# Pooled attention into a gated MLP: PSUM banks by turns in blocks 5 to 8, operands on one address remainder, and a new order of the steps

## The chip, the cores and the metric

The kernel runs on one core of one Trainium2 chip. Its time is the device time of one execution in microseconds (us), and a kernel's time is the median of several executions. Profiles, waits and clocks come from one further execution under the hardware profiler.

## The reference

```python
k_p = k.reshape(B, H, Sp, 8, D).mean(axis=3)          # B, H, S, D = 8, 8, 576, 64; Sp = 72
v_p = v.reshape(B, H, Sp, 8, D).mean(axis=3)
scores = q @ k_p.T / sqrt(D)
attn = exp(scores - max) / (sum + 1e-9)
x = (attn @ v_p) as 4608 tokens x 512
xn = x / sqrt(mean(x*x) + 1e-6) * rms_g
g, val = xn @ w_gate, xn @ w_val                      # 512 -> 1536 each
out = (g * sigmoid(g) * val) @ w_out                  # 1536 -> 512
```

All in float32.

## The kernel before, in words

The 4608 tokens are handled in nine blocks of 512 tokens (block 0 to block 8). The attention of a batch (576 tokens) is worked out in four pairs of heads and gives the tokens of about one block; it runs ahead of the MLP blocks that use it. The hidden width of 1536 is cut into twelve tiles f of 128 (written 0 to 9, a, b).

Accuracy comes from splitting: every float32 operand y of the MLP is stored as y_hi (rounded to float32r) and y_lo = y - y_hi, and a product is made of three float32r matmuls: hi x hi, lo x hi, hi x lo. All big matmuls have a 128x128 stationary operand and 512 moving columns.

**Blocks 0 to 4.** For each tile f: `mm1` twice (steps mg and me, 12 matmuls each, line 812; stationary the weights W1, moving the tokens xh, xl), which fill PSUM banks 2 and 3; `gate` (gt, ScalarE Silu out of bank 2), `val` (vl, VectorE product with bank 3), `act_hi` (hi, ScalarE, line 834), `act_lo` (lo, VectorE, line 839), then `mm2` (mo, 12 matmuls, line 853; stationary the activation hh or hl, moving the weights W2), which accumulates four output tiles in banks 4 to 7 over all twelve f. After the last tile `o_copy` (ev, line 867) takes the banks out and `o_store` (st) sends them to memory.

**Blocks 5 to 8.** They are worked in two pairs, (5, 6) and (7, 8), and the first projection of a pair is done for both blocks at once by seven half-size products a tile in place of eight (steps pr`<i><f><k>`, k = 0 to 6, six matmuls each, function `product`, line 764). X collects products 0, 2 and 4 in one PSUM bank (px), Y the products 1, 3, 5 and 6 in another (py). VectorE and ScalarE combine them (cp, u2, sa, u3, c2, sw, v2, v1, va, vb, lines 908 to 917): `v1` and `va` make the odd block's activation from product 6, the last one; `vb` leaves the even block's activation in an SBUF tile `hb` that holds all twelve tiles. The odd block's `mm2` of tile f is done in two halves (mp) among the products of tile f+1; that of the last tile (mo5b, mo7b) follows the last product. Then the even block has only its twelve `mm2` (mo60 to mo6b, mo80 to mo8b) from the stored `hb`.

**PSUM.** The eight banks are given by number: attention in banks 0 and 1, X in 2, Y in 3, output tiles of every block in 4 to 7 (lines 756, 758, 844). A step such as `av730:1` overrides the bank.

**SBUF.** Tiles are laid out pool after pool, each rounded up to 32 bytes a partition. `const.tile([P, 104])` on line 208, named "rest", is read by nobody and takes 416 bytes a partition. In this layout the start addresses, taken by 256, leave these remainders: the weights W1, W2 and the split tokens xp of blocks 5 to 8 (which lie in freed W1 slots) 0; xh, xl, the ring of eight buffers for the products' weights, act, hl and the pool tile "st" 128; hh and the transposed probabilities 192.

**hh and hl.** hh has two buffers; hl has one, and for odd f of an even block (6, 8) `act_lo` uses the one act buffer in place of it (line 837).

**The order of the work** is written out by hand in two strings, `ORDER` (block 0 and the attention it needs) and `LATER` (all else, 2072 steps). The function `run` issues the steps one after the other; each engine executes its own in that order, and SyncE issues all DMAs in that order too. The attention's steps are sc (scores, PE), mx, sb, sm (VectorE), ex (ScalarE Exp), nm (GpSimd), tr (VectorE transpose), dm (12 DMAs that place the transposed probabilities), av (PE), xc, xd (copies), sq, jn (squares and their sum); the token norm's are sh, sl, rm (PE), rt (ScalarE Sqrt), rc (VectorE reciprocal, line 540), rs (VectorE scaling, line 547); the pair's operands are made by ys, yh, yl; rl loads a product's weights.

Of the kernel before, what the change touches and what calls it, by code (L numbers as in the profile page):

```python
# [92 lines left out]
sm221 wf03 ex220 wd0 wh03 sm220 wl01 lv23 nm221 ws01 av210:0 gt14 nm220 pk23 av211:1 wl03 me14 lq23 xd21 xc210 ws03
xc211 mo13 vl14 hi14 pv23 wh04 wl04 mg15 lo14 ws04 wh02 wl02 sc23:01 ws02 sq21 tr22 gt15 jn21 me15 dm22 mx230 sb230
mx231 ex230 sb231 mo14 vl15 ex231 sm230 hi15 lo15 nm230 sm231 mg16 nm231 lk30 tr23 me16 gt16 dm23 av220:0 vl16
av221:1 pk30 xc220 hi16 mo15 xd22 xc221 sq22 lo16 jn22 mg17 lq30 lv30 wt1 me17 gt17 wf10 sc30:01 vl17 wd1 wf11 wh11
hi17 pv30 wl11 mo16 lk31 wh13 wf12 ws11 mx301 lv31 wl13 lo17 wf13 ws13 mx300 mg18 sb300 sb301 ex300 av230:0 ex301
# [15 lines left out]
sb421 sb420 ex421 pv42 me28 gt28 sm421 nm421 mo27 ex420 vl28 lk43 hi28 sm420 lv43 wt5 mg29 lo28 pk43 nm420 av410:0
lq43 gt29 wf50 av411:1 wf51 me29 wd5 xd41 xc410 wf52 pv43 xc411 wh53 wf53 wh51 wl53 sq41 sc43:01 vl29 wl51 ws53 hi29
jn41 ws51 mo28 mx431 lk50 mx430 lo29 mg2a wh52 wl52 wh54 wl54 ws52 ws54 tr42 me2a gt2a sb431 dm42 pk50 ex431 sb430
mo29 vl2a ex430 sm431 hi2a sm430 nm431 lo2a mg2b nm430 tr43 me2b dm43 gt2b mo2a xh33 vl2b xh31 xl33 xh32 xl31 xh30
av420:0 xl32 hi2b av421:1 xl30 xc420 xc421 lo2b mg30 lv51 kt3 lq50 xd42 lv50 me30 gt30 sc50:01 vl30 pv50 hi30 mo2b
lk51 mx501 lo30 wd6 mx500 sb500 mg31 ev21 ev22 ex500 sb501 st21 st22 pk51 lq51 ex501 av430:0 sm500 gt31 av431:1
sm501 nm500 me31 xd43 nm501 xc430 pv51 xc431 ev23 sq42 tr50 st23 jn42 ev20 dm50 vl31 mo30 sq43 hi31 jn43 lo31 mg32
sh4 sl4 rm40:0 gt32 rm41:1 me32 rt40 st20 rt41 rc40 lv52 wt6 sc51:01 vl32 mo31 lk52 rs40 hi32 wf60 wf61 wh61 wl61  # L120
wh63 lo32 mg33 wl63 ws61 rc41 wf62 ws63 wf63 me33 rs41 gt33 mx511 wh62 wh64 sb511 wl62 mo32 vl33 ex511 wl64 ws62
mx510 sb510 ws64 pk52 hi33 av500:0 sm511 ex510 lq52 av501:1 xc500 lo33 nm511 mg34 xc501 xd50 sm510 sq50 wd7 pv52
# [835 lines left out]
```

## Time and profile before

| | |
|---|---|
| median of 3 runs | 1043.09 us (1041.45 to 1043.99) |
| the profiled execution: its time, its span | 1040.0 us, 1037.9 us |
| mean granted TensorE clock | 0.976 |
| busy: PE, DVE (VectorE), ACT (ScalarE), POOL (GpSimd) | 1007.0, 632.0, 449.3, 227.4 us |

PE's rows are TensorE's matmuls, PEld its weight loads. In a row of the timeline the columns are: start, duration in us, engine, line, operation, tile written <- tiles read, shape, count, and in brackets the idle time of the engine just before with what ended it. The duration of one matmul in the profile (about 0.4 us) covers its way through the array; matmuls follow one another much closer than that, so their pace is read from start to start.

### The profile page before, as it was taken

The page shows a single profiled execution, that of the slowest core. Times are in us where ns is not written, and L with a number is a line of the kernel's source. Part 1 is how long each engine was busy: PE and PEld are TensorE (multiplying, and loading weights), DVE is VectorE, ACT ScalarE, POOL GpSimd, SP SyncE. Part 2 cuts the span into 40 slices and gives each one's busy share as a digit, 9 for nine tenths or more (in the row PEclk, how much of TensorE's full clock was granted, in tenths as well). Part 3 has the DMA queues.
Part 4 walks back from the last instruction along what each step waited for, and adds up shares of the span by engine and source line. Part 5 has one row for each costly group of instructions (what it writes and reads, how often), then busy time and mean ns, then how long its engine had stood idle before and what let it go on. Part 6 is the DMA issues. An engine that isn't in the chain of part 4 may idle for free.

```text
span 1037.9 us, 13861 instructions
## 1 busy us (share of the span) xinstructions
PE 1007.0 (97%) x4850; PEld 790.9 (76%) x4850; DVE 632.0 (61%) x1024; ACT 449.3 (43%) x845; POOL 227.4 (22%) x216
## 2 busy tenths in 40 slices
PE   7999999999999999999999999999999999999987
PEld 6777777777777777777777787878786778888866
DVE  6699996554772964775485385644655764444432
ACT  5767665543473454554364362322333432111121
POOL 2314440144333541355324140000000000000000
PEclk7599999999999999999999999999999999999999
DMA  9345422245345353444244323564544134544311
GB/s 303 126 158 187 171 73 77 71 139 143 102 134 156 100 159 91 140 145 150 83 146 147 97 89 115 162 206 143 167 143 134 41 122 146 151 149 144 102 40 41
DMA packets 97077, 134.71 MB, mean 130 GB/s; under 512 B 10225, under 2 KB 60145, under 8 KB 95729
## 3 DMA queue, kind: packets, MB, share of 16 engines
q1 hardware_dynamic: 97008, 133.83, 41.3%
q8 instruction: 39, 0.64, 0.2%
q14 instruction: 30, 0.24, 0.1%
HBM read 91.23 MB, written 34.60 MB: 121 GB/s over the span
## 4 chain that ended last, share of the span: by engine, by line
PE 86%; DVE 7%; ACT 2%; issue 2%; DMA 1%; SPq 0%; ACTq 0%; DVEq 0%
PE psg L812 28%; PE po L853 26%; PE py L764 13%; PE px L764 10%; PE pss L390 4%; PE psx L471 3%; DVE wt L258 1%; PE pst L447 1%; DVE wt L262 1%; DMA main<-kT 1%; PE psr L555 1%; DVE wt L254 1%; DVE w L280 0%; ACT prob L368 0%; PE psb L579 0%
## 5 line engine op out<-in xcount | busy, mean ns | idle before, releaser
L812 PE MATMUL psg<-xh,w 128*128 128x512 f32 x960 | 304.4, 399 | 1.8 <-ACT act L819 1.8
L853 PE MATMUL po<-w,hh 128*128 128x512 f32 x864 | 227.4, 395 | 0.0
L812 PEld LDWEIGHTS psg<-xh,w 128*128 128x128 f32 x960 | 177.4, 188 | 50.7 <-issue 5.3
L853 PEld LDWEIGHTS po<-w,hh 128*128 128x128 f32 x864 | 163.9, 190 | 36.8
L812 PE MATMUL psg<-xl,w 128*128 128x512 f32 x480 | 189.3, 395 | 0.2 <-DVE xl L642 0.2
L764 PE MATMUL py<-xp,wp 128*128 128x512 f32 x576 | 149.7, 395 | 0.8 <-DVE u L914 0.8
L853 PE MATMUL po<-w,hl 128*128 128x512 f32 x432 | 126.9, 403 | 9.8 <-DVE hl L839 5.1
L764 PEld LDWEIGHTS py<-xp,wp 128*128 128x128 f32 x576 | 108.3, 188 | 27.2 <-DVE u L914 1.2
L764 PE MATMUL px<-xp,wp 128*128 128x512 f32 x432 | 112.7, 396 | 0.0
L812 PEld LDWEIGHTS psg<-xl,w 128*128 128x128 f32 x480 | 90.2, 188 | 21.9 <-DVE xl L642 0.6
L853 PEld LDWEIGHTS po<-w,hl 128*128 128x128 f32 x432 | 79.8, 189 | 34.0 <-DVE hl L839 6.5
L421 POOL TENSOR_TENSOR prob<-prob,sm 128x360 f32<-128x360 f32 x48 | 43.7, 911 | 282.4 <-DVE sm L417 279.9
L764 PEld LDWEIGHTS px<-xp,wp 128*128 128x128 f32 x432 | 81.0, 188 | 20.0 <-ACT xraw L479 0.5
L824 DVE TENSOR_TENSOR act<-act,psg 128x512 f32<-128x512 f32 x60 | 40.8, 681 | 81.7 <-PE psg L812 70.1
L834 ACT CAST hh<-act 128x512 fp32r<-128x512 f32 x84 | 52.1, 621 | 66.0 <-DVE act L824 57.2
L839 DVE TENSOR_TENSOR hl<-act,hh 128x512 fp32r<-128x512 f32 x78 | 58.3, 748 | 34.3 <-ACT hh L834 26.7
L819 ACT ACTIVATE act<-psg 128x512 f32<-128x512 f32 x60 | 35.8, 597 | 67.7 <-PE psg L812 64.1
L819 ACT ACT_TABLE_LOAD x34 | 43.6, 1283 | 38.0 <-DVE hl L839 19.9
L911 DVE TENSOR_TENSOR u<-u,py 128x512 f32<-128x512 f32 x24 | 16.5, 688 | 67.4 <-PE py L764 67.4
L516 POOL TENSOR_TENSOR acc<-acc,sq 128x576 f32<-128x576 f32 x21 | 31.5, 1499 | 102.4 <-ACT sq L510 102.4
L913 ACT ACTIVATE hb<-hb 128x512 f32<-128x512 f32 x24 | 15.2, 632 | 87.8 <-DVE hb L912 87.8
L686 POOL TENSOR_TENSOR wt<-wsum,wt 128x256 fp32r<-128x256 f32 x48 | 38.3, 814 | 53.1 <-ACT wt L682 53.0
(132 smaller groups left out, 1225.0 us busy)
## 6 DMA issues: line engine op xcount, KB each, us to landing
wp<-sum SPq DMA_DIRECT2D x96, 256.0 KB
wp<-blocks SPq DMA_DIRECT2D x72, 256.0 KB
blocks<-w SPq DMA_DIRECT2D x24, 512.0 KB
sum<-wt SPq DMA_DIRECT2D x48, 256.0 KB
wx<-w SPq DMA_DIRECT2D x10, 1024.0 KB
v<-vN SPq DMA_DIRECT2D x32, 288.0 KB
out<-o SPq DMA_DIRECT2D x36, 256.0 KB
wx<-w SPq DMA_DIRECT2D x16, 512.0 KB
```

Of the source, the lines that this page charges most:

```text
L390: nc.tensor.matmul(s["ps", h][:, t * SP:(t + 1) * SP], s["q"][r, o:o + P], s["pk"][r, :], start=True, stop=True)
L421: nc.gpsimd.tensor_tensor(l_pr(h), l_pr(h), sm[:, :, None].broadcast_to([P, len(OFFS2), SP]), ALU.mult)
L471: nc.tensor.matmul(ps[r, :n], s["pv"][:, r], x, start=True, stop=True)
L516: nc.gpsimd.tensor_add(acc[b], acc[b], st[b, p]["sq"])
L686: nc.gpsimd.tensor_sub(y[:, 1], place(f, f"T{k}"), y[:, 0].bitcast(F32))
L764: nc.tensor.matmul(ps[:, :NB], w[:, a, c, :], x[:, b, c, :], start=j == 0 and not more, stop=j == len(todo) - 1, skip_group_check=more)
L812: nc.tensor.matmul(ps[:, :NB], w[:, c, cols], x[c], start=(j == 0), stop=(j == len(todo) - 1))
L819: nc.scalar.activation(t, ps[:, :NB], AF.Silu)
L824: nc.vector.tensor_mul(t, t, ps[:, :NB])
L834: nc.scalar.copy(a, act_in(i, f))
L839: eng.tensor_sub(l, act_in(i, f), hh[i, f].bitcast(F32))
L853: nc.tensor.matmul(po[i][t], x[i, f][:, t * P:(t + 1) * P], w, start=(f == 0 and k == 0), stop=(f == NF - 1 and k == 2))
```

## The change

Three things are changed. No step is added or taken out: `LATER` holds the same 2072 steps.

1. **Banks by turns.** X and Y of pair (7, 8) go to banks 4 and 5; the output tiles of block 6 go to banks 0 to 3, those of block 7 to 6, 7, 0, 1 and those of block 8 to 2 to 5. The even block's first step, mo60 or mo80, now stands ahead of the odd block's last step mo5b or mo7b, with its hi60/lo60 (hi80/lo80) among the products of the last tile. `act_lo` of an even block's tile 0 goes to a buffer of the pool tile "st".
2. **Addresses.** The unused "rest" tile is gone (416 bytes less ahead of everything), `pk` is padded from 72 to 96 elements (2 buffers, 96 bytes more each) and the four tiles "mxe" from 80 to 128 bytes (32 bytes more each after rounding). The start addresses by 256 become: W1, W2 and xp 0 - 416, xh, xl, ring, act, hl and "st" 128 - 416 + 128, hh 192 - 416 + 128 + 192. All of these leave the remainder 96.
3. **A new order.** The first 29 steps of `LATER` are the same; from there on it differs. In blocks 1 to 4 the attention's steps stand at other places among the tiles. The attention of batch 7 is done by tile 4 of block 5 (before: by the end of block 5), its token norm (rm7 to rs7) in tile 5 of block 5 (before: during mo60 to mo64), and half of the operands yh7, yl7 are made in the last tile of block 5.

```diff
+BANK1 = {5: (2, 3), 7: (4, 5)}
+BANK2 = {6: (0, 1, 2, 3), 7: (6, 7, 0, 1), 8: (2, 3, 4, 5)}
...
-    const.tile([P, 104], F32, name="rest")
...
-            pk = sb2.tile([P, SP], F32, tag="pk", name=f"pk{b}_{p}")
+            pk = sb2.tile([P, 96], F32, tag="pk", name=f"pk{b}_{p}")[:, :SP]
...
-            x = sb1.tile([P, 2, 2, n], F32, tag=f"mxe{p}", name=f"mx{b}_{p}")
-            s["mx"], s["sm"] = x[:, 0], x[:, 1]
+            x = sb1.tile([P, 2, 2, 8], F32, tag=f"mxe{p}", name=f"mx{b}_{p}")
+            s["mx"], s["sm"] = x[:, 0, :, :n], x[:, 1, :, :n]
...
-            st["X"] = bank(2, f"px{i}_{f}_{k}")
+            st["X"] = bank(BANK1[i][0], f"px{i}_{f}_{k}")
         elif k in (1, 3, 5):
-            st["Y"] = bank(3, f"py{i}_{f}_{k}")
+            st["Y"] = bank(BANK1[i][1], f"py{i}_{f}_{k}")
...
     def act_lo(i, f, eng):
-        tag = "act" if second(i) and f % 2 else "hl"
-        l = hl[i, f] = sb1.tile([P, NB], F32R, tag=tag, name=f"hl{i}_{f}")
+        if second(i) and f == 0:
+            l = sb2.tile([P, NB], F32R, tag="st", name=f"hl{i}_{f}")
+        else:
+            l = sb1.tile([P, NB], F32R, tag="act" if second(i) and f % 2 else "hl", name=f"hl{i}_{f}")
+        hl[i, f] = l
...
-            po[i] = [bank(4 + t, f"po{i}_{t}") for t in range(NB // P)]
+            po[i] = [bank(k, f"po{i}_{t}") for t, k in enumerate(BANK2.get(i, (4, 5, 6, 7)))]
```

The order at the end of block 5, before and after:

```
... pr5b5 c25b rl705 sw5b mp5a1 rl706 v25b vb5b pr5b6 av730:0 rl710 v15b av731:1 va5b xc730 xc731 xd73 hi5b sq73 lo5b
jn73 mo5b hi60 lo60 sh7 sl7 mo60 hi61 ev52 ev51 ev50 st52 ev53 st51 lo61 st50 st53 rm71:0 hi62 rm70:1 mo61 ...

... u25b hi60 mp5a0 ... pr5b3 lo60 ... c25b pr5b5 sw5b yl72 mp5a1 rl706 v25b vb5b pr5b6 mo60 rl710 v15b va5b
hi5b lo5b mo5b hi61 lo61 mo61 hi62 ev52 ev53 ev50 st52 ev51 st53 lo62 st50 st51 mo62 ...
```

and in tile 5 of block 5, after:

```
pr550 rl560 v154 va54 rm70:1 rl561 cp55 rm71:0 pr551 hi54 rt71 lo54 pr552 rl562 u255 rt70 rc71 mp540 rl563 sa55 pr553 rc70
pr554 rl564 u355 rl565 c255 pr555 rs70 sw55 mp541 rl566 v255 vb55 pr556 rs71 pr560 ...
```

More of the change, by code (lines that the diff above doesn't have):

```diff
@@ L93 @@
[L93 to L97, printed above, removed]
@@ L113 @@
[L113 to L117, printed above, removed]
@@ L118 @@
[L118 to L122, printed above, removed]
@@ L163 @@
-nm731 mp591 rl5b6 v25a sw5a tr73 pr5a6 dm73 vb5a pr5b0 v15a va5a pr5b1 cp5b hi5a pr5b2 lo5a u25b mp5a0 sa5b pr5b3
-rl700 pr5b4 rl701 u35b rl702 rl703 rl704 pr5b5 c25b rl705 sw5b mp5a1 rl706 v25b vb5b pr5b6 av730:0 rl710 v15b
-av731:1 va5b xc730 xc731 xd73 hi5b sq73 lo5b jn73 mo5b hi60 lo60 sh7 sl7 mo60 hi61 ev52 ev51 ev50 st52 ev53 st51
-lo61 st50 st53 rm71:0 hi62 rm70:1 mo61 rt71 lo62 rt70 rc71 mo62 hi63 lo63 rc70 mo63 hi64 lo64 rs70 mo64 hi65 lo65
-rs71 mo65 hi66 ys73 yh72 yh71 lo66 yl72 mo66 hi67 yh73 lo67 yl71 yh70 mo67 hi68 yl70 lo68 ys74 mo68 hi69 lo69 yh74
@@ L183 @@
-pr7a3 pr7a4 rl7b4 u37a pr7a5 rl7b5 c27a sw7a mp791 rl7b6 v27a vb7a pr7a6 pr7b0 v17a va7a pr7b1 cp7b hi7a pr7b2 lo7a
-u27b mp7a0 sa7b pr7b3 pr7b4 u37b pr7b5 c27b sw7b mp7a1 v27b vb7b pr7b6 v17b va7b hi7b lo7b mo7b hi80 lo80 mo80 hi81
-ev72 ev71 ev70 st72 ev73 st71 lo81 st70 st73 mo81 hi82 lo82 mo82 hi83 lo83 mo83 hi84 lo84 mo84 hi85 lo85 mo85 hi86
-lo86 mo86 hi87 lo87 mo87 hi88 lo88 mo88 hi89 lo89 mo89 hi8a lo8a mo8a hi8b lo8b mo8b ev83 ev82 ev81 ev80 st83 st82
-st81 st80
+pv22 dm21 me13 gt13 wt0 sc22:01 wf00 vl13 wf01 wh01 hi13 mo12 mx220 wf02 wh03 sb220 wf03 lo13 ex220 wl01 wd0 mx221
@@ new lines @@
+mx320 sb320 mx321 ex320 sb321 me20 lk33 lv33 gt20 sm320 ws24 nm320 mo1b ex321 vl20 pk33 hi20 sm321 lq33 mg21 ev13
+ev12 nm321 st13 lo20 st12 tr32 me21 gt21 dm32 ev10 ev11 av310:0 vl21 av311:1 xc310 hi21 mo20 xd31 xc311 pv33 lo21
+sq31 sc33:01 jn31 st11 mg22 st10 mx330 lk40 mx331 sb331 lv40 wt3 sb330 ex331 me22 gt22 sm331 wd3 wf30 nm331 av320:0
+pk40 ex330 wf31 av321:1 vl22 lq40 wf32 mo21 xd32 hi22 wf33 sm330 xc321 wh34 lo22 nm330 xc320 pv40 wh32 wl34 mg23
+wl32 ws34 sq32 ws32 jn32 me23 gt23 wh31 wh33 wl31 mo22 vl23 wl33 ws31 hi23 ws33 tr33 mg24 lo23 lv41 dm33 sc40:01
@@ new lines @@
+gt24 me24 mx401 mx400 sb400 sb401 ex400 mo23 vl24 ex401 lk41 sm400 hi24 sm401 nm400 mg25 lo24 nm401 tr40 pk41 dm40
+av330:0 gt25 av331:1 me25 xd33 xc330 pv41 xc331 sq33 mo24 vl25 jn33 hi25 lo25 sh3 mg26 lq41 sl3 wd4 wt4 rm30:0 gt26
+lv42 rm31:1 me26 rt30 wf40 rt31 rc30 wf41 wh41 av400:0 wf42 wh43 av401:1 xc400 wf43 vl26 mo25 xc401 wl43 rs30 hi26
+wl41 ws43 ws41 lo26 mg27 xd40 rc31 pv42 wh44 sc41:01 gt27 wl44 rs31 me27 ws44 lk42 wh42 wl42 mx410 sq40 sb410 ws42
+mo26 mx411 ex410 vl27 sb411 hi27 sm410 ex411 mg28 lo27 nm410 sm411 pk42 nm411 me28 lq42 gt28 tr41 dm41 mo27 vl28
@@ new lines @@
+hi28 lo28 sc42:01 mg29 mx421 sb421 mx420 ex421 sb420 lk43 lv43 me29 gt29 sm421 wt5 ex420 av410:0 vl29 av411:1 pk43
+nm421 mo28 hi29 sm420 lq43 wf50 xc410 wd5 xc411 xd41 wf51 lo29 wh51 nm420 wh53 pv43 mg2a wl53 wf52 ws53 sq41 wl51
+jn41 ws51 sc43:01 gt2a wf53 me2a lk50 mx430 mx431 wh52 mo29 wh54 wl52 vl2a wl54 hi2a ws52 pk50 ws54 lo2a lq50 mg2b
+tr42 sb430 dm42 sb431 ex430 me2b gt2b sm430 nm430 mo2a xh33 vl2b xh32 xl33 xh30 xl32 xh31 xl30 lv50 hi2b xl31 ex431
+lo2b mg30 kt3 sm431 nm431 av420:0 gt30 tr43 av421:1 me30 xd42 dm43 xc420 pv50 xc421 sq42 sc50:01 vl30 jn42 hi30 mo2b
@@ new lines @@
+mx500 mx501 lo30 sb500 sb501 ex500 mg31 ev20 lk51 ev22 st20 ex501 st22 sm500 wd6 me31 sm501 wt6 gt31 lv51 pk51 ev23
+nm500 av430:0 lq51 vl31 ev21 st23 av431:1 wf60 hi31 st21 mo30 nm501 xd43 xc430 xc431 wf61 lo31 wf62 wf63 mg32 pv51
+me32 wh63 gt32 wl63 wh61 ws63 wl61 ws61 mo31 vl32 hi32 lo32 wh62 mg33 wl62 wh64 ws62 wl64 ws64 sq43 tr50 me33 jn43
+gt33 dm50 sh4 sl4 mo32 vl33 hi33 lo33 rm40:0 rm41:1 rt40 mg34 lv52 rt41 rc40 me34 gt34 rs40 av500:0 wt7 vl34 av501:1
+xc500 rc41 hi34 mo33 xc501 wf70 lo34 wf71 wh71 xd50 rs41 wl71 mg35 wh73 wl73 ws71 wd7 wf72 pv52 sq50 ws73 wf73
@@ new lines @@
+mo38 xc520 hi39 lo39 wh82 av521:1 wh83 wl82 mg3a xc521 xd52 wl83 ws82 pv60 ws83 sq52 jn52 tr53 me3a gt3a dm53
+sc60:01 vl3a hi3a mo39 mx600 mx601 lo3a sb601 sb600 ex601 mg3b lk61 ex600 lv61 sm601 me3b sm600 nm601 gt3b nm600
+tr60 av530:0 xh43 vl3b dm60 av531:1 xh41 xl43 mo3a xh42 xl41 xh40 xl42 hi3b xl40 xc530 xc531 lo3b mg40 xd53 pv61
+pk61 sq53 me40 gt40 jn53 lq61 wd9 sh5 lv62 wt9 mo3b sl5 kt4 vl40 wf90 hi40 rm50:0 ev30 rm51:1 ev31 wf91 mg41 lo40
+rt50 st30 wf92 st31 wf93 rt51 rc50 me41 gt41 ev32 rc51 ev33 st32 sc61:01 st33 vl41 mo40 lk62 mx611 hi41 sb611 wh94
@@ new lines @@
+lo41 ex611 wl94 rs51 av600:1 ws94 mg42 wh93 xc600 wl93 mx610 sm611 ws93 sb610 nm611 av601:1 wh92 pk62 gt42 wl92 me42
+rs50 lq62 ws92 xc601 wh91 pv62 ex610 wl91 mo41 vl42 ws91 xd60 hi42 sm610 sq60 lo42 nm610 mg43 tr61 dm61 sc62:01 gt43
+me43 mx620 mx621 wta sb621 sb620 ex621 mo42 vl43 wfa0 ex620 sm621 hi43 wfa1 sm620 wha1 nm621 lk63 wha3 mg44 lo43
+nm620 wda wla3 lv63 wfa2 wsa3 me44 wfa3 gt44 wla1 pk63 wsa1 lq63 av610:0 vl44 av611:1 xc610 hi44 mo43 xd61 xc611
+lo44 pv63 mg45 wha2 wha4 wla2 wla4 wsa2 wsa4 sq61 tr62 sc63:01 gt45 jn61 dm62 me45 mx630 sb630 mx631 ex630 sb631
@@ new lines @@
+mo44 vl45 ex631 sm630 hi45 lo45 nm630 sm631 mg46 nm631 lk70 lv70 me46 gt46 tr63 dm63 mo45 vl46 hi46 pk70 lo46
+av620:0 av621:1 xc620 mg47 xc621 xd62 pv70 lq70 me47 gt47 lv71 sq62 jn62 av630:0 vl47 av631:1 xc630 wdb hi47 mo46
+xd63 xc631 lo47 pv71 mg48 sq63 wtb sc70:01 gt48 jn63 me48 lk71 mx700 wfb0 sb700 sh6 mx701 wfb1 ex700 sl6 wfb2 mo47
+sb701 wfb3 whb3 vl48 ex701 wlb3 sm700 hi48 wsb3 whb2 sm701 nm700 rm60:0 mg49 lo48 wlb2 rt60 pk71 nm701 wsb2 lq71
+tr70 whb1 rm61:1 wlb1 gt49 rc60 me49 dm70 rt61 rs60 mo48 whb4 vl49 wlb4 rc61 hi49 sc71:01 lo49 mg4a mx710 wsb4 wsb1
@@ new lines @@
+rs61 lk72 lv72 me4a ys53 gt4a ys54 yh52 mo49 vl4a yh51 yl52 hi4a yh50 mg4b lo4a yl51 yh53 yh54 yl50 me4b gt4b yl53
+yl54 mo4a rl500 rl501 ys56 rl502 rl503 rl504 rl505 vl4b yh56 rl506 ys55 rl510 pr500 hi4b pr501 lo4b rl511 cp50 yh55
+yl56 pr502 rl512 u250 mp4b0 yl55 rl513 sa50 mx711 pr503 sb711 pk72 ex711 pr504 rl514 u350 lq72 sb710 av700:1 rl515
+c250 ex710 av701:0 sm711 xc700 sw50 pr505 sm710 nm711 xd70 mp4b1 nm710 rl516 v250 xc701 sq70 vb50 pr506 ev41 ev40
+pv72 st41 pr510 st40 rl520 v150 sc72:01 va50 rl521 cp51 tr71 hi50 pr511 lk73 lo50 ev43 lv73 dm71 mx720 pr512 ev42
@@ new lines @@
+pr533 sq72 dm73 pr534 u353 jn72 pr535 c253 sw53 mp521 v253 vb53 pr536 pr540 v153 va53 rl544 pr541 cp54 rl545 hi53
+rl546 rl550 pr542 lo53 rl551 rl552 u254 mp530 rl553 sa54 pr543 av730:1 rl554 u354 av731:0 xc730 pr544 xc731 xd73
+sq73 pr545 jn73 rl555 c254 sw54 mp531 rl556 v254 sh7 vb54 pr546 sl7 pr550 rl560 v154 va54 rm70:1 rl561 cp55 rm71:0
+pr551 hi54 rt71 lo54 pr552 rl562 u255 rt70 rc71 mp540 rl563 sa55 pr553 rc70 pr554 rl564 u355 rl565 c255 pr555 rs70
+sw55 mp541 rl566 v255 vb55 pr556 rs71 pr560 rl570 v155 rl571 cp56 va55 pr561 hi55 pr562 lo55 rl572 u256 mp550 rl573
@@ new lines @@
+sa56 pr563 pr564 rl574 u356 pr565 rl575 c256 sw56 mp551 rl576 v256 vb56 pr566 pr570 rl580 v156 va56 pr571 rl581 cp57
+hi56 pr572 lo56 rl582 u257 mp560 rl583 sa57 pr573 pr574 rl584 u357 pr575 rl585 c257 sw57 mp561 rl586 v257 vb57 pr576
+pr580 rl590 v157 va57 pr581 rl591 cp58 hi57 pr582 lo57 rl592 u258 mp570 rl593 sa58 pr583 pr584 rl594 u358 pr585
+rl595 c258 sw58 mp571 rl596 v258 vb58 pr586 pr590 rl5a0 v158 va58 pr591 rl5a1 cp59 hi58 pr592 lo58 rl5a2 u259 mp580
+rl5a3 sa59 pr593 pr594 rl5a4 u359 pr595 rl5a5 c259 sw59 mp581 rl5a6 v259 vb59 pr596 pr5a0 rl5b0 v159 va59 pr5a1
@@ new lines @@
+rl5b1 cp5a hi59 pr5a2 lo59 rl5b2 u25a mp590 rl5b3 sa5a pr5a3 pr5a4 rl5b4 u35a pr5a5 rl5b5 c25a sw5a mp591 rl5b6 v25a
+vb5a pr5a6 pr5b0 rl700 v15a va5a pr5b1 rl701 cp5b hi5a pr5b2 yh70 lo5a rl702 u25b hi60 mp5a0 yl70 rl703 sa5b yh71
+pr5b3 lo60 yl71 pr5b4 rl704 u35b rl705 yh72 c25b pr5b5 sw5b yl72 mp5a1 rl706 v25b vb5b pr5b6 mo60 rl710 v15b va5b
+hi5b lo5b mo5b hi61 lo61 mo61 hi62 ev52 ev53 ev50 st52 ev51 st53 lo62 st50 st51 mo62 hi63 lo63 mo63 hi64 lo64 ys73
+mo64 hi65 lo65 yh73 ys74 mo65 hi66 yl73 yh74 lo66 yl74 mo66 hi67 lo67 ys76 mo67 hi68 ys75 yh76 lo68 yh75 yl76 mo68
@@ new lines @@
+rl780 v176 va76 pr771 rl781 cp77 hi76 pr772 lo76 rl782 u277 mp760 rl783 sa77 pr773 pr774 rl784 u377 pr775 rl785 c277
+sw77 mp761 rl786 v277 vb77 pr776 pr780 rl790 v177 va77 pr781 rl791 cp78 hi77 pr782 lo77 rl792 u278 mp770 rl793 sa78
+pr783 pr784 rl794 u378 pr785 rl795 c278 sw78 mp771 rl796 v278 vb78 pr786 pr790 rl7a0 v178 va78 pr791 rl7a1 cp79 hi78
+pr792 lo78 rl7a2 u279 mp780 rl7a3 sa79 pr793 pr794 rl7a4 u379 pr795 rl7a5 c279 sw79 mp781 rl7a6 v279 vb79 pr796
+pr7a0 rl7b0 v179 va79 pr7a1 rl7b1 cp7a hi79 pr7a2 lo79 rl7b2 u27a mp790 rl7b3 sa7a pr7a3 pr7a4 rl7b4 u37a pr7a5
@@ L188 @@
+rl7b5 c27a sw7a mp791 rl7b6 v27a vb7a pr7a6 pr7b0 v17a va7a pr7b1 cp7b hi7a pr7b2 lo7a u27b hi80 mp7a0 sa7b lo80
+pr7b3 pr7b4 u37b pr7b5 c27b sw7b mp7a1 v27b vb7b pr7b6 mo80 v17b va7b hi7b lo7b mo7b hi81 lo81 mo81 hi82 ev70 ev71
+ev72 st70 ev73 st71 lo82 st72 st73 mo82 hi83 lo83 mo83 hi84 lo84 mo84 hi85 lo85 mo85 hi86 lo86 mo86 hi87 lo87 mo87
+hi88 lo88 mo88 hi89 lo89 mo89 hi8a lo8a mo8a hi8b lo8b mo8b ev83 ev82 ev81 ev80 st83 st82 st81 st80
 """
```

103 lines of the change are left out of this document (31 added, 72 removed).

## The prediction

> **What bounds the kernel now.** I read the page first, then what TensorE waited for, then the timeline of TensorE around its longest waits, and the chain of waits for the pace of a matmul.
>
> ```profile
> span 1037.9 us, 13861 instructions
> PE 1007.0 (97%) x4850; PEld 790.9 (76%) x4850; DVE 632.0 (61%) x1024; ACT 449.3 (43%) x845; POOL 227.4 (22%) x216
> ...
> PE 86%; DVE 7%; ACT 2%; issue 2%; DMA 1%; SPq 0%; ACTq 0%; DVEq 0%
> ```
>
> TensorE is busy for 97% of the span and carries 86% of the chain that ended last. So there are only two ways to a shorter time: fewer stalls of TensorE, or a quicker pace of its matmuls. The stalls after block 0 are few; what PE waited for (total us, times, longest):
>
> ```profile
> PE po L853 <- DVE hl L839: 5.1, 3, 2.9
> PE po L853 <- DVE o L867: 4.7, 3, 2.2
> ...
> PE py L764 <- DVE u L914: 0.8, 1, 0.8
> ```
>
> The first two rows belong to `mm2`, and nearly all of them lies at two places, the ends of blocks 5 and 7. TensorE's timeline there:
>
> ```profile
> 796.32 1.56 PE L764 MATMUL py<-xp,wp 128*128 128x512 f32 x6
> 797.81 1.19 PE L471 MATMUL psx<-pt,pv 72*64 72x256 f32 x8
> 800.76 0.50 PE L853 MATMUL po<-w,hl 128*128 128x512 f32 x1 [1.76 <-DVE hl L839]
> ...
> 806.06 0.50 PE L853 MATMUL po<-w,hl 128*128 128x512 f32 x1 [2.24 <-DVE o L867]
> ...
> 810.50 0.69 PE L533 MATMUL psr<-sums,ones 128*128 128x288 f32 x4
> 811.03 1.08 PE L853 MATMUL po<-w,hl 128*128 128x512 f32 x4
> ```
>
> ```profile
> 988.68 1.56 PE L764 MATMUL py<-xp,wp 128*128 128x512 f32 x6
> 993.12 0.50 PE L853 MATMUL po<-w,hl 128*128 128x512 f32 x1 [2.88 <-DVE hl L839]
> ...
> 998.68 0.50 PE L853 MATMUL po<-w,hl 128*128 128x512 f32 x1 [1.19 <-DVE o L867]
> ...
> 1001.55 1.09 PE L853 MATMUL po<-w,hl 128*128 128x512 f32 x4
> ```
>
> Each place shows the last product (pr5b6, pr7b6), a wait for the odd block's last hl, mo5b or mo7b, and then a second wait, for the odd block's output tiles to be copied out of banks 4 to 7, before mo60 or mo80 can begin. And the work between and after the waits is slow, because the granted clock falls (columns: stretch, length, busy time of PE, PEld, DVE, ACT, POOL, then PEclk):
>
> ```profile
> 808.00:810.50 2.50, 2.50 (x7) 1.94 (x7) 0.00 (x0) 0.00 (x0) 0.00 (x0) 0.57 0.37 141
> 995.00:997.00 2.00, 2.00 (x6) 1.39 (x5) 0.27 (x1) 0.00 (x0) 0.00 (x0) 0.50 0.00 0
> ```
>
> The Trainium skill (TensorE: Matmul & The Clock Gate, "HAM oscillation — how this bites in real kernels") puts the idle gap that costs the clock above about 3.4 us; the rows show it lost after gaps of 2.88 us, and of 1.76 and 2.24 us with one tile's work between, so the measurement decides.
>
> **Part 1, the banks.** What mo5b waits for does not change: product 6 of the last tile is read by v1, then va, hi, lo. The chain at the end of block 7, where nothing else is in it, on VectorE and, for hi, on ScalarE:
>
> ```profile
> 990.28 0.69 DVE L915 TENSOR_TENSOR u<-u,py 128x512 f32<-128x512 f32 x1 [1.29 <-PE py L764]
> 991.00 0.69 DVE L916 TENSOR_TENSOR act<-act,u 128x512 f32<-128x512 f32 x1
> 992.38 0.69 DVE L839 TENSOR_TENSOR hl<-act,hh 128x512 fp32r<-128x512 f32 x1 [0.68 <-ACT hh L834]
> ```
>
> ```profile
> 991.73 0.62 ACT L834 CAST hh<-act 128x512 fp32r<-128x512 f32 x1 [4.26 <-DVE act L916]
> ```
>
> The pace of the work that can stand before it, from the chain of waits (start, us, what):
>
> ```profile
> 627.86 2.76 PE po L853 x12
> 630.62 5.59 PE psg L812 x24
> ...
> 661.29 1.40 PE px L764 x6
> ```
>
> After the change mo60 (12 matmuls, 2.76 us) follows product 6 at once. Product 6 issues for 1.40 us, so in block 5 mo60 would stand from 797.72 to 800.48, and mo5b can start when its hl is there, as before at 800.76: a stall of 0.28. It ends at 803.5 and mo61 begins, which before began at 811.03. That is 7.5 less. At block 7: 988.68 + 1.40 + 2.76 = 992.84, hl at 993.12, mo81 at 995.9 in place of 1001.55: 5.65 less. The lost clock is within these differences; with 0.28 us idle I expect none to be lost.
>
> What mo60 needs is there: hi60 and lo60 read `hb`, made by vb5b or earlier ones long before, and lo60 has a buffer of its own in "st", whose last user is the squares of batch 7. Banks 0 and 1 were last used for the token norm of tile 5. Banks 2 and 3 are X and Y of the last tile: bank 3 is read by v1 until 0.9 us after product 6, and mo60 comes to it after nine matmuls, at 2.1 us. mo61 needs hi61 and lo61: hi61 waits for the hh buffer that mo60 frees (0.62 us after that it is done), lo61 for lo5b and hi61; 1.4 us in all, within mo5b's 2.8. The new waits put ev and lo62 behind them on ScalarE and VectorE, again within a step of PE.
>
> Two things were free in the first gap and now are not: batch 7's last av and the norm's psr. What an av pair costs within running products:
>
> ```profile
> 677.84 1.56 PE L764 MATMUL py<-xp,wp 128*128 128x512 f32 x6
> 679.33 1.19 PE L471 MATMUL psx<-pt,pv 72*64 72x256 f32 x8
> 680.45 1.67 PE L764 MATMUL px<-xp,wp 128*128 128x512 f32 x6
> ```
>
> 677.84 + 1.40 = 679.24, the next product starts at 680.45 and its first matmul is 0.1 longer: 1.3 us. The psr stood between 810.50 and 811.03, 0.5, with a switch 0.6. Block 5: 7.5 - 1.3 - 0.6 = 5.6 less. Sum of part 1: **-11.2 us**. The 0.8 us behind L914 in the first tile of block 7 stays, since no mo stands there.
>
> **Part 2, the addresses.** The rows of the chain above show two paces: `mm1` takes 5.59/24 = 232.9 ns a matmul, the products 1.40/6 = 233, `mm2` only 2.76/12 = 230.0. In `mm1` and in the products the start of the moving operand and that of the stationary one differ by 128 in the address modulo 256; in two of three matmuls of `mm2` the stationary one is hh, 64 off. The change makes all differences 0, which no row shows for 512 columns. The counts:
>
> ```profile
> L812 PE MATMUL psg<-xh,w 128*128 128x512 f32 x960 | 304.4, 399 | 1.8 <-ACT act L819 1.8
> ...
> L812 PE MATMUL psg<-xl,w 128*128 128x512 f32 x480 | 189.3, 395 | 0.2 <-DVE xl L642 0.2
> L764 PE MATMUL py<-xp,wp 128*128 128x512 f32 x576 | 149.7, 395 | 0.8 <-DVE u L914 0.8
> ...
> L764 PE MATMUL px<-xp,wp 128*128 128x512 f32 x432 | 112.7, 396 | 0.0
> ```
>
> 2448 matmuls of `mm1` and products. If distance matters and 0 is at least as good as 64, they gain 2.9 ns each: -7 us. If each step of 64 is worth 2.9 ns, they gain 5.8 and the 1296 of `mm2` gain 2.9: -18 us. If the pace has another cause, 0. If equal starts are what collides, and distance helps, the mirror image: 2448 x 2.9 + 1296 x 5.8 = +15 us. I take **-7**, the value of the nearest row, since nothing shows that a distance of 0 reaches beyond it. Starts off a multiple of 64 bytes (96 is one) are new for 512 columns, but not for the scores, whose moving operand pk lies at remainder 128 and 160 by turns, first at 128, then at 160:
>
> ```profile
> 291.21 1.34 PE L390 MATMUL pss<-pk,q 64*128 64x72 f32 x20
> ...
> 435.97 1.34 PE L390 MATMUL pss<-pk,q 64*128 64x72 f32 x20
> ```
>
> Both take 1.34, so I charge nothing for that.
>
> **Part 3, the order.** The step count is equal, and TensorE has slack nowhere, so the order can only make or remove stalls. One it may remove lies where block 3's first mo waits for block 2's output copies:
>
> ```profile
> 426.88 1.19 PE L853 MATMUL po<-w,hl 128*128 128x512 f32 x4 [1.29 <-DVE o L867]
> ```
>
> In the new order VectorE's steps between mo2b and mo30 are fewer (5.6 us instead of 8.5, added from their rows), so I take -1.3. One it may add is tile 5 of block 5, which now holds the whole norm of batch 7:
>
> ```profile
> L547 DVE SCALAR_TENSOR_TENSOR xraw<-xraw,gcol,acc 128x288 f32<-128x288 f32 x48 | 28.7, 657 | 0.1
> ...
> L540 DVE RECIPROCAL acc<-acc 128x288 f32<-128x288 f32 x12 | 23.3, 1939 | 9.7 <-ACT acc L537 9.6
> L911 DVE TENSOR_TENSOR u<-u,py 128x512 f32<-128x512 f32 x24 | 16.5, 688 | 67.4 <-PE py L764 67.4
> L537 ACT ACT_TABLE_LOAD x6 | 7.7, 1283 | 1.7 <-PE psr L533 1.6
> ```
>
> VectorE has 8 x 0.69 of the tile's own, 8 scalings x 0.60 (28.7/48) and 2 reciprocals x 1.94: 14.2 us, while PE has 7 x 1.40 + 2.76 + 0.6 = 13.2. Two table loads of 1.28 us on ScalarE stand before the reciprocals and before sa. u3, v2 and v1 queue behind these blocks of 2 us, and product 5, 6 and the next tile's product 1 write Y only after them: +1.0 from the sum, up to 4 if each of the three waits; I take +2. The attention of batch 7 moves from all twelve tiles of block 5 into its first five. VectorE's load in those twelve tiles was:
>
> ```profile
> 640.00:800.00 160.00, 159.00 (x734) 126.48 (x732) 83.49 (x138) 49.72 (x77) 7.88 (x8) 1.00 0.53 163
> ```
>
> 83.5 of 160 us on VectorE; in the new order its rows add up to 9 to 13 us of each of the first five tiles' 14 to 15 us, so it still fits, but with little room. The 12 DMAs a pair queue on SyncE behind ring loads and have about a tile of products until av needs them; GpSimd (7.9 of 160 us) has room for nm and jn. The rest I leave at 0, with 3 us to both sides. Sum: **+0.7**.
>
> **The sum.** 1040.0 - 11.2 - 7 + 0.7 = 1022.5 by the profiled execution's time. That lies 3.1 below the median of the runs, 1043.1, so I forecast **1025.6** for the median.
>
> **The rivals.** (B) The address remainder does nothing: 1043.1 - 11.2 + 0.7 = 1032.6. For it: `mm2` differs from the others in more than the address. The Trainium skill says so (SBUF — State Buffer, "Who interferes with whom"): TensorE's read port for the moving operand and that for the weights are independent. The two paces are against it, without settling it. (C) The steps go on to 0: 1043.1 - 10.5 - 18 = 1014.6. (D) The crowded blocks stall: VectorE's added steps from tile 9 of block 4 to tile 1 of block 5 come to 52 us beside 55 of PE, so a few longer ones make PE wait; 8 us there and at tile 5, and no help of the addresses, give 1043.1 - 11.2 + 8 = 1039.9. (E) Slower: equal starts collide. At +15 the time is 1043.1 - 10.5 + 15 = 1047.6. It outweighs the banks from 10.5/3744 = 2.8 ns a matmul on. For it speaks that no row has a distance of 0; against it that the nearer distance is now the quicker one. That the banks do not do what they say is small: both waits named in the profile are released by steps that no longer stand ahead of mo60.
>
> **How the numbers follow.** A measurement can tell about 0.3%, 3.1 us. Forecast 0.38, B 0.27, C 0.17, D 0.08, E 0.10. A, B and C are faster (0.82) and D in one case of four (0.02), else within 0.3% (0.06): faster 0.84, same 0.06, slower 0.10. The range takes in B and D above and C with its 3 us of the order and a little more below: 1009 to 1041; it leaves out E and the tail of C, 0.15 or so.
>
> **What would show it.** Right: mo60 directly behind pr5b6, one stall of about 0.3 before mo5b and mo7b, no wait of po on o at these places, clock 1.00 from 800 us on; psg x24 at 5.5 or less, px x6 at 1.38 or less. Wrong: psg x24 unchanged (B) or at 5.65 or more (E), waits of py or px on u, hb or act in block 5 (D), or a wait of po on hl above 1 us with mo60 done.

## The result, and the profile after

| | before | after |
|---|---|---|
| median | 1042.74 us (4 runs, 1041.45 to 1043.99) | 1013.63 us (4 runs, 1011.95 to 1017.04) |
| ratio, 95% interval | | 0.9725 [0.9695, 0.9755] |
| profiled execution: time, span, mean granted clock | 1040.0, 1037.9, 0.976 | 1014.67, 1012.9, 0.979 |

The change makes the kernel faster by 29.1 us, 25.3 by the two profiled executions. 1025.6 was forecast, with a range of 1009 to 1041. The head of the page after:

```profile
span 1012.9 us, 13861 instructions
PE 989.6 (98%) x4850; PEld 788.0 (78%) x4850; DVE 633.1 (63%) x1024; ACT 455.8 (45%) x851; POOL 225.4 (22%) x216
```

The instructions are as many as before, and TensorE is still the bound. Its busy time fell by 17.4 us: the same 4850 matmuls are done quicker. What PE waited for in the products and in `mm2` (total us, times, longest):

```profile
PE py L765 <- DVE u L918: 1.1, 2, 0.8
PE po L857 <- DVE hl L843: 0.9, 3, 0.5
```

A row of po waiting for o, 4.7 us before, is no longer among them, and the waits for hl went from 5.1 to 0.9. TensorE's timeline at the ends of blocks 5 and 7:

```profile
788.63 1.67 PE L765 MATMUL py<-xp,wp 128*128 128x512 f32 x6 [0.28 <-DVE u L918]
790.14 0.39 PE L857 MATMUL po<-w,hl 128*128 128x512 f32 x1
...
793.24 0.50 PE L857 MATMUL po<-w,hl 128*128 128x512 f32 x1 [0.19 <-DVE hl L843]
...
796.09 1.07 PE L857 MATMUL po<-w,hl 128*128 128x512 f32 x4
```

```profile
969.88 1.52 PE L765 MATMUL py<-xp,wp 128*128 128x512 f32 x6
971.24 0.39 PE L857 MATMUL po<-w,hl 128*128 128x512 f32 x1
...
974.35 0.50 PE L857 MATMUL po<-w,hl 128*128 128x512 f32 x1 [0.22 <-DVE hl L843]
...
977.20 1.07 PE L857 MATMUL po<-w,hl 128*128 128x512 f32 x4
```

In each, the first row is the last product, the second the start of mo60 or mo80, which follows it at once; then come mo5b or mo7b after one short stall, and mo61 or mo81. From the last product's start to mo61 it is 7.46 us, where it was 14.71 (796.32 to 811.03); to mo81 7.32, where it was 12.87. (The 14.71 held batch 7's last av and psr too, which now stand elsewhere.) The clock there (stretch, length, busy time of PE, PEld, DVE, ACT, POOL, then PEclk):

```profile
793.00:795.00 2.00, 1.81 (x9) 1.47 (x9) 0.88 (x2) 0.62 (x1) 0.00 (x0) 1.00 0.00 0
972.00:976.00 4.00, 3.78 (x17) 2.83 (x16) 2.65 (x5) 1.24 (x2) 0.00 (x0) 1.00 0.00 0
```

It stays at 1.00, where it fell to 0.57 and 0.50. And the pace, from the chain of waits (start, us, what):

```profile
243.44 5.44 PE psg L813 x24
...
345.43 2.72 PE po L857 x12
...
650.12 1.36 PE px L765 x6
```

All three kinds now take the same time: 5.44/24 = 2.72/12 = 1.36/6 = 226.7 ns a matmul. Before, `mm1` and the products took 233 and `mm2` 230.

### The profile page after: what moved, and what is told of

The parts are those of the page before. It is cut to its first block, busy times and chain, and to the rows that moved or that the text cites. A ratio compares the mean times of both kernels' runs of the same rounds, so it can differ in the third digit from the quotient of the medians.

```text
span 1012.9 us, 13861 instructions
## 1 busy us (share of the span) xinstructions
PE 989.6 (98%) x4850; PEld 788.0 (78%) x4850; DVE 633.1 (63%) x1024; ACT 455.8 (45%) x851; POOL 225.4 (22%) x216
## 4 chain that ended last, share of the span: by engine, by line
PE 85%; DVE 8%; ACT 3%; issue 2%; DMA 1%; SPq 0%; ACTq 0%; DVEq 0%
PE psg L813 28%; PE po L857 26%; PE py L765 13%; PE px L765 10%; PE pss L391 4%; PE psx L472 3%; DVE wt L259 2%; DVE wt L263 1%; DVE wt L255 1%; DMA main<-qT 1%; DVE w L281 1%; ACT prob L369 1%; PE psr L556 1%; DMA out<-o 1%; PE pst L448 0%
## 5 line engine op out<-in xcount | busy, mean ns | idle before, releaser
L813 PE MATMUL psg<-xh,w 128*128 128x512 f32 x960 | 301.0, 395 | 2.0 <-ACT act L820 2.0
L857 PE MATMUL po<-w,hh 128*128 128x512 f32 x864 | 223.0, 390 | 0.0
L813 PE MATMUL psg<-xl,w 128*128 128x512 f32 x480 | 186.7, 390 | 0.0
L765 PE MATMUL py<-xp,wp 128*128 128x512 f32 x576 | 147.5, 391 | 1.2 <-DVE u L918 1.1
L857 PE MATMUL po<-w,hl 128*128 128x512 f32 x432 | 124.6, 397 | 1.0 <-DVE hl L843 0.9
L765 PE MATMUL px<-xp,wp 128*128 128x512 f32 x432 | 110.1, 390 | 0.0
L912 ACT COPY hb<-px 128x512 f32<-128x512 f32 x24 | 14.1, 587 | 87.8 <-PE px L765 87.8
L915 DVE TENSOR_TENSOR u<-u,py 128x512 f32<-128x512 f32 x24 | 16.4, 685 | 58.3 <-PE py L765 58.3
L917 ACT ACTIVATE hb<-hb 128x512 f32<-128x512 f32 x24 | 15.2, 632 | 81.4 <-DVE hb L916 81.4
```

The costliest lines, as they stand in the source:

```text
L765: nc.tensor.matmul(ps[:, :NB], w[:, a, c, :], x[:, b, c, :], start=j == 0 and not more, stop=j == len(todo) - 1, skip_group_check=more)
L813: nc.tensor.matmul(ps[:, :NB], w[:, c, cols], x[c], start=(j == 0), stop=(j == len(todo) - 1))
L857: nc.tensor.matmul(po[i][t], x[i, f][:, t * P:(t + 1) * P], w, start=(f == 0 and k == 0), stop=(f == NF - 1 and k == 2))
```

## The experiments

The theory after the result: the banks and the order give what was forecast, some 10.5, and the addresses over twice as much as forecast, since the pace at distance 0 lies beyond the nearest row. Its rival: the addresses give 7 or a little more, and the banks, the order and the clock the other 20. The first four kernels cut the change into its parts; all are compared with before in one sitting, where it had a median of 1042.96 in 16 runs (1038.8 to 1046.0).

**1. The addresses alone**, on the kernel before:

```diff
-    const.tile([P, 104], F32, name="rest")
...
+            pk = sb2.tile([P, 96], F32, tag="pk", name=f"pk{b}_{p}")[:, :SP]
...
+            x = sb1.tile([P, 2, 2, 8], F32, tag=f"mxe{p}", name=f"mx{b}_{p}")
```

> The kernel before with the three layout edits alone (no rest tile, pk and mxe padded): old banks, old order. Theory (the pace depends on the distance of the two operands' starts modulo 256): 12 matmuls of mm1 or mm2 in 2.72 us, 6 of a product in 1.36, as in the changed kernel, the gaps at the ends of blocks 5 and 7 unchanged; 2448 matmuls 5.6 ns quicker and 1296 of mm2 about 3, so -17 us, 1025.5. Rival (the pace came from the new order or the banks, as two matmuls that write the same bank in turn): pace as before, 1042 to 1043.

Measured: 1028.44 us (1027.32 to 1030.08), ratio 0.9869 [0.9843, 0.9895], or -14.5 us. Its chain has the pace of the whole change, and its waits the stalls of before:

```profile
244.21 5.44 PE psg L811 x24
...
357.64 2.72 PE po L852 x12
...
648.85 1.36 PE px L763 x6
```

```profile
PE po L852 <- DVE hl L838: 5.2, 3, 2.9
PE po L852 <- DVE o L866: 4.8, 3, 2.3
```

So the theory holds, not its rival, and three small edits of the layout are worth half of the gain. From all start-to-start times of the two traces the quicker pace should give 16.8 us. It gave less, 11.4 by the profiled executions (1040.0 to 1028.6), because it was worth nothing in blocks 0 and 1: block 2's first `mm1` starts at 292.48 before and at 293.75 here. Their share of the 16.8, two ninths, is 3.7, and they end 1.3 later: 16.8 - 3.7 - 1.3 = 11.8. In block 0 TensorE waits for others (164.51 us busy of 176, PEclk 0.88 before). In block 1, this execution lost the clock after a gap of 2 us:

```profile
184.68 1.08 PE L811 MATMUL psg<-xh,w 128*128 128x512 f32 x2 [1.98 <-ACT act L818]
```

```profile
185.00:188.00 3.00, 3.00 (x8) 2.32 (x8) 1.81 (x6) 1.94 (x3) 0.42 (x1) 0.50 0.00 0
```

The changed kernel has the same gap, and there the clock stayed:

```profile
185.52 0.73 PE L813 MATMUL psg<-xh,w 128*128 128x512 f32 x2 [1.98 <-ACT act L820]
```

```profile
185.60:188.00 2.40, 2.40 (x11) 1.96 (x12) 1.24 (x3) 2.18 (x3) 0.00 (x0) 1.00 0.00 0
```

Of two gaps of 1.98 us, one cost the clock (8 matmuls in 3 us) and one did not (11 in 2.4).

**2. All but the addresses**: the changed kernel with the three layout edits taken back.

```diff
+    const.tile([P, 104], F32, name="rest")
...
+            pk = sb2.tile([P, SP], F32, tag="pk", name=f"pk{b}_{p}")
...
+            x = sb1.tile([P, 2, 2, n], F32, tag=f"mxe{p}", name=f"mx{b}_{p}")
```

> The changed kernel with the old layout (rest tile back, pk and mxe unpadded): new banks and new order alone. Theory: 24 matmuls of mm1 in 5.59 us again, stalls of 0.2 to 0.3 us before mo5b and mo7b, clock 1.00 there; -11 us from the kernel before, 1031.5. If banks and order are worth more than I reckoned, under 1029; if the new order costs as much as it brings, 1036 or more.

Measured: 1028.78 us (1027.89 to 1032.24), ratio 0.9878 [0.9854, 0.9902], or -14.2 by the medians and -10.9 by the spans of the profiled executions (1037.9 to 1027.0). The pace of before is back:

```profile
262.74 5.60 PE psg L814 x24
...
346.78 2.76 PE po L858 x12
...
666.74 1.40 PE px L766 x6
```

With it the ends of the blocks can be measured at before's pace. The last product, mo5b and mo61; then the last product, mo7b and mo81:

```profile
798.20 1.66 PE L766 MATMUL py<-xp,wp 128*128 128x512 f32 x6 [0.24 <-DVE u L919]
...
802.80 0.51 PE L858 MATMUL po<-w,hl 128*128 128x512 f32 x1
...
805.72 1.10 PE L858 MATMUL po<-w,hl 128*128 128x512 f32 x4
```

```profile
983.43 1.56 PE L766 MATMUL py<-xp,wp 128*128 128x512 f32 x6
...
987.93 0.51 PE L858 MATMUL po<-w,hl 128*128 128x512 f32 x1 [0.15 <-DVE hl L844]
...
990.85 1.10 PE L858 MATMUL po<-w,hl 128*128 128x512 f32 x4
```

7.52 us in place of 14.71 and 7.42 in place of 12.87: 7.2 and 5.45 less. The two halves add up: by the medians -14.5 and -14.2 against -29.1 for the whole, by the profiled executions -11.4 and -11.2 against -25.3.

**3. One block's banks, in the old order**: on before, the output tiles of block 8 go to banks 0 to 3, and hi80, lo80 and mo80 stand ahead of the odd block's last tile.

```diff
+            po[i] = [bank(t if i == 8 else 4 + t, f"po{i}_{t}") for t in range(NB // P)]
...
+        if (i, f) == (8, 0):
+            l = sb2.tile([P, NB], F32R, tag="st", name=f"hl{i}_{f}")
...
+... u27b hi80 mp7a0 sa7b pr7b3 lo80 ... pr7b6 mo80 v17b va7b hi7b lo7b mo7b hi81 ev72 ev71 ev70 st72 ev73 st71 lo81 ...
```

> The kernel before with one edit: block 8's output tiles in banks 0 to 3, hi80, lo80 and mo80 ahead as in the change, lo80 in a buffer of st. Old layout, old order else. Theory: the gap at the end of block 7 shrinks from 2.88 and 1.19 us with a lost clock to one of 0.3, -5.6 us, 1037.1. Rival (mo80 only moves the wait to mo81, whose hh buffer and hl come later): a new stall of 1 us or more before mo81, -3 us or less.

Measured: 1038.37 us (11 runs, 1036.16 to 1040.62), ratio 0.9964 [0.995, 0.9979], or -4.6 us by the medians and -3.8 by the profiled executions (1040.0 to 1036.16). The starts of the last product, of mo7b and of mo81:

```profile
989.13 1.56 PE L762 MATMUL py<-xp,wp 128*128 128x512 f32 x6
...
993.62 0.50 PE L854 MATMUL po<-w,hl 128*128 128x512 f32 x1 [0.17 <-DVE hl L840]
...
997.96 1.20 PE L854 MATMUL po<-w,hl 128*128 128x512 f32 x4 [1.28 <-DVE hl L840]
```

The first wait shrank to 0.17, but a new one of 1.28 stands before mo81: from the last product to mo81 it is 8.83 us, where experiment 2 has 7.42 at the same pace. So of the gain of 5.45 about 1.4 is lost. lo81 follows the output copies ev72, ev71 and ev70 in the old order and waits behind those of them that are VectorE's. The changed order puts lo81 ahead of them, and there mo81 does not wait: the banks give their full gain only with that. Block 6 could not be done in the same way: in the old order the last av and the norm's sums of batch 7 still use banks 0 and 1 there. The new order has finished them by tile 5 of block 5.

**4. The banks without the early mo60 and mo80**: the changed kernel, with mo60 and mo80 back behind mo5b and mo7b, and their hi and lo steps behind lo5b and lo7b (the order at the end of block 5; block 7 is done likewise).

```diff
-... pr5b6 mo60 rl710 v15b va5b hi5b lo5b mo5b hi61 lo61 mo61 ...
+... pr5b6 rl710 v15b va5b hi5b lo5b hi60 lo60 mo5b mo60 hi61 lo61 mo61 ...
```

> The changed kernel with hi60, lo60, mo60 and hi80, lo80, mo80 put back behind lo5b, mo5b and lo7b, mo7b; banks by turns, layout and the rest of the order kept. Theory (the filling of the chain v1, va, hi, lo is worth about as much as the freed banks): gaps of 2.9 us before mo5b and mo7b come back and with them some us at half clock, mo60 and mo80 follow at once; 2.6 + 1 to 1.5 us at each place, +7 to +8 us, 1021. Rival (the old loss was the wait for the copies out of the banks): +1 us or less at each place, 1014 to 1016.

Measured: 1021.87 us (1015.76 to 1025.39), ratio 0.9799 [0.9766, 0.9832], or 8.2 more than the change. The starts of mo5b and mo7b:

```profile
793.35 0.50 PE L856 MATMUL po<-w,hl 128*128 128x512 f32 x1 [2.88 <-DVE hl L842]
...
977.15 0.50 PE L856 MATMUL po<-w,hl 128*128 128x512 f32 x1 [2.88 <-DVE hl L842]
```

The two waits of 2.88 are what mo60 and mo80 fill. The clock behind the first (behind the second it reads 1.00 too):

```profile
793.00:796.00 3.00, 2.65 (x12) 2.20 (x13) 0.89 (x2) 0.09 (x1) 0.00 (x0) 1.00 0.00 1
```

In this execution it was not lost, where the same 2.88 at the end of block 7 had cost it before. The span was 1018.4, 5.5 above the change's: twice 2.88 less the change's short stalls. The kernel's four executions took 1015.76, 1020.19, 1023.55 and 1025.39 us at mean granted clocks of 0.986, 0.981, 0.976 and 0.974. So these executions of one and the same kernel are the longer the lower their clock, and a gap of 2.88 us lost it in the kernel before and not here. This kernel's times spread by 9.6 us and the change's by 5.1; that the two gaps make the difference is likely, but only the one execution was seen in a trace.

The other six kernels ask what it is in the addresses. All are the changed kernel with tiles added that nobody reads; the first was measured in five runs, the others in one each, beside nine runs of before (1039.5 to 1045.1). A single time is worth a few us here, so the argument goes by the paces in the traces.

**5. Is it the remainder 96, or that all are equal?** 160 bytes ahead of everything make every remainder 0:

```diff
+    const.tile([P, 40], F32, name="rest")
```

> The changed kernel with an unused tile of 160 bytes back in the first pool: all operands at remainder 0 in place of 96, distances still 0. Theory (only the distance counts): 24 matmuls of mm1 in 5.44 us, time as the changed kernel, 1012 to 1016. Rival (the common remainder counts, 96 itself or a start off a multiple of 64): another pace, by 1 ns a matmul 4 us.

Measured: 1013.98 us (1012.24 to 1017.09), ratio 0.9739 [0.9713, 0.9764], the change's time, with its pace:

```profile
261.26 5.44 PE psg L814 x24
```

Remainder 0 is as good as 96; what the two kernels share is that the starts are equal.

**6. Many distances at once**: 32 bytes between each two of the eight buffers that hold xh, xl and the ring.

```diff
+        if steps_made:
+            sb1.tile([P, 8], F32, tag=f"step{len(steps_made)}", name=f"step{len(steps_made)}")
+        steps_made.append(1)
```

> The changed kernel with 32 unused bytes between the eight buffers that hold xh, xl and the products' weights, so that in mm1 the moving operand starts 0, 32, 64, 96, 128, 160, 192 or 224 bytes (modulo 256) beyond W1, and in the products the stationary one does so beyond xp; hh and hl are 224 beyond W2. Theory (the pace falls off with the distance, the shorter way round): 226.7 ns a matmul at 0, 228.3 at 32 and 224, 229.8 at 64 and 192, 231.3 at 96 and 160, 232.8 at 128; some 9 us over the changed kernel, 1022. Rival (only an equal start is quick, and all others share one slow pace of 230 to 233): 226.7 in one buffer alone. Second rival (it has a direction): 32 to 96 unlike 224 to 160.

Measured: 1028.07 us, and every kind is slow, not only those far apart:

```profile
232.41 5.57 PE psg L822 x24
...
335.79 2.80 PE po L866 x12
```

```profile
674.58 1.40 PE py L765 x6
```

The products use the ring's buffers in turn, so their matmuls can be sorted by distance. The mean from start to start within a product, by (next stationary start less moving start) modulo 256: 0: 229 ns; 32: 232.9; 64: 233.5; 96: 234; 128: 232.9; 160: 232.7; 192: 230.6; 224: 233.3. That is no slope from 128 down to 0, as the steps of 64 in the forecast's largest case had it. Almost all distances cost the same, and two are better; at 0 the median is 227, as in the change.

**7. Only hh away**: 128 unused bytes (two buffers of 64) ahead of the hh buffers, so that hh alone stands 128 off W2.

```diff
+        if not hh:
+            sb2.tile([P, 16], F32, tag="gap", name="gap")
```

> The changed kernel with 128 unused bytes before hh, so that hh starts 128 from W2 modulo 256 and nothing else moves. Theory (address alone; that mm2 was quicker than mm1 in the kernel before had no other cause): the eight hh matmuls of mm2 go from 1.81 us to 1.86, 12 matmuls of mm2 from 2.72 to 2.77, 864 x 5.5 ns = +4.7 us, 1018. Rival (mm2 is quicker by its kind): 2.72 stays.

Measured: 1021.85 us. `mm1` keeps its pace, and `mm2` loses it:

```profile
244.24 5.44 PE psg L813 x24
...
346.73 2.77 PE po L859 x12
...
697.73 1.39 PE py L765 x6
```

`mm2` has the same instructions and the same order as in the change, so its own pace was a matter of its address, not of its kind. The product in the last row takes 1.39 though its own operands agree; it follows directly on a matmul of hh. The trace tells how far this goes. Sorted by the stationary operands of a matmul and of the next one, the mean from start to start (pairs up to 300 ns apart) is 232.9 ns from hh to hh, 232.3 from another operand to hh and 234.5 from hh to another, and 228.0 where neither is hh (in the change 227.6, 227.7, 226.7 and 227.5). From hl to hl it is 228.5, as in the change (228.4). So the time is lost where hh is the stationary operand of a matmul or of the one behind it.

**8. to 10. A gap between W1 and W2 on the one side and xh, xl, the ring, hh and hl on the other**, of 256, 64 and 32 bytes:

```diff
+    sb1.tile([P, 64], F32, tag="gap", name="gap")
```

(16 and 8 elements in the other two.)

> The changed kernel with 256 unused bytes between the weights' pool and all pools after it: W1, W2 and xp stay, xh, xl, the ring, act, hl, hh move by 256. Theory (the remainder by 256 decides): 24 matmuls of mm1 in 5.44 us, 6 of a product in 1.36, no change. Rival (the rule is by 512 or more, since all distances were multiples of 512 until now): 5.5 us or more.

> The same with 64 bytes: in mm1 the stationary operand starts 64 ahead of the moving one (192 modulo 256), in the products and in mm2 64 beyond it. After the scan I hold that only an equal start is quick and that there is a direction: mm1 at 229.8 ns as hh had it before (24 in 5.51 us), products and mm2 at 233.5 as the scan's products at 64 (6 in 1.40, 12 in 2.80). Rival (the old theory of distance either way round): both at 229.8.

> The same with 32 bytes. After the scan (products at 32: 232.9, mm2 at 224: 233.2) both kinds are as slow as at 128: 24 of mm1 in 5.58 us, 6 of a product in 1.40, 12 of mm2 in 2.80; time some 1033. Rival (nearer is quicker): 228.3 ns a matmul, 5.48, 1.37 and 2.74.

Measured: 1013.06 us with 256, 1029.12 with 64 and 1032.57 with 32. The chain's rows in this order of kernels:

```profile
260.50 5.44 PE psg L814 x24
```

```profile
262.15 5.51 PE psg L814 x24
...
374.31 2.80 PE po L858 x12
...
655.26 1.40 PE px L766 x6
```

```profile
262.77 5.60 PE psg L814 x24
```

256 bytes change nothing, so what counts is the address modulo 256. With 64, in `mm1` the stationary W1 lies 64 before the moving operand, and a matmul takes 5.51/24 = 229.6 ns; in `mm2` and the products the stationary operand lies 64 beyond the moving one, and a matmul takes 233.3. So the distance has a direction, as the scan had shown (192: 230.6, 64: 233.5). hh of before lay 64 before W2 (192 against 256, that is 0), and had 230. With 32, `mm1` takes 5.60/24 = 233.3, as much as with 128.

## Why the prediction was right, and where its sum was off

The direction, the mechanism of the banks and the range hold; the forecast itself was 12 us too slow. By its own steps:

**What bounds the kernel**: right. The two ways named, fewer stalls and a quicker pace, are the two halves of the gain.

**Part 1, the banks**: right. Before mo5b and mo7b the forecast leaves a stall of 0.28; worked out in the same way (start of mo5b less start of mo60 less 12 matmuls) it is 793.24 - 790.14 - 2.72 = 0.38, and 0.39 in block 7. Counted from the last product, mo61 and mo81 come 7.2 and 5.45 earlier at the old pace (experiment 2), 7.5 and 5.65 forecast. The clock stayed at 1.00. That mo60 and mo80 have to stand ahead for this is shown by experiment 4, and that lo81 has to stand ahead of the copies by experiment 3.

**Part 3, the order**: the stalls lie where the forecast put them, but less of the first is removed and the second costs less. mo30's row has no idle time before it, where it had 1.29:

```profile
422.51 1.55 PE L857 MATMUL po<-w,hl 128*128 128x512 f32 x4
423.90 0.40 PE L857 MATMUL po<-w,hh 128*128 128x512 f32 x1
```

But its four matmuls take 1.39 us from start to start, where four at the pace of 226.7 ns take 0.91: mo30 starts earlier and then waits inside the row. In experiment 2 the same wait is counted with 0.7 us and released by ScalarE's output copy, not VectorE's. So of the 1.3 that was to go some 0.5 stays.

The full tile 5 of block 5, for which +2 was taken:

```profile
709.59 1.52 PE L765 MATMUL px<-xp,wp 128*128 128x512 f32 x6
711.11 1.66 PE L765 MATMUL py<-xp,wp 128*128 128x512 f32 x6
...
714.22 1.66 PE L765 MATMUL py<-xp,wp 128*128 128x512 f32 x6
...
717.33 1.66 PE L765 MATMUL py<-xp,wp 128*128 128x512 f32 x6
718.82 1.52 PE L765 MATMUL px<-xp,wp 128*128 128x512 f32 x6
```

The three rows of py are products 5 and 6 and the next tile's product 1, the three that the forecast named. Each is late and has a longer first matmul. From product 4 at 709.59 to the next tile's product 2 at 718.82 stand six groups of six matmuls, 1.36 each: 9.23 us in place of 8.16, so 1.1 is lost of the 2 that was taken. The last tile of block 5 has a stall that was not forecast, 0.28 before its last product (its row is the first of the timeline after). Case D, the crowded blocks, came to less than 2 us of its 8. By profiled executions parts 1 and 3 together gave 1028.82 - 1040.0 = -11.2 (experiment 2), with -10.5 forecast; by medians it is -14.2, with an interval of 10.2 to 15.2.

**Part 2, the addresses**: the step that failed is "I take **-7**, the value of the nearest row, since nothing shows that a distance of 0 reaches beyond it". From experiment 2 to the change, which differ in nothing else, it is 1014.67 - 1028.82 = -14.2 by profiled executions; before against experiment 1 has -11.4 by profiled executions and -14.5 by medians, with an interval of 11.0 to 16.4. The term's sign and its subject were right and its size was about half of what it is: the pace at 0 is 226.7, 3.3 below the nearest row's 230.0, and so `mm2` gains too, which -7 left out.

**Case C** gave 1014.6, within 1.0 of what was measured, but for a wrong reason. Its steps of 64 would put a distance of 32 between those of 0 and 64; experiment 10 has 233.3 there, as much as at 128. What the runs show is one quick place, 0, with half of the gain left at 64 on one side.

**Case B**, that the remainder does nothing, is refuted by experiments 1, 7 and 10: with the same instructions, 32 bytes more between the two operands made 226.7 ns into 233.3. What makes it so, no run shows. The Trainium skill's rule behind this case (SBUF — State Buffer, "Who interferes with whom") is that TensorE's two read ports are independent. By that alone the distance would cost nothing; the measurement differs, and it decides. **Case E**, that equal starts collide, had the sign wrong: they are the quick ones.

**From the profiled execution to the median**: +3.1 was added, the distance of before's. The change's median lies 1.0 below its profiled execution. The step took for a property of the program what is in the main chance of one execution: the 16 executions of before in the sitting of experiment 1 lie between 1038.8 and 1046.0, and 1040.0 is near their lower end. The sum with what was measured: 1040.0 - 11.2 - 14.2 - 1.0 = 1013.6.

What stays open is why the clock is lost after a gap in one execution and not in another. So what the removed gaps cost beyond their length can't be given as one number.
